# Polysketch attention and feed-forward on one core: GpSimd issues V and all input-projection weights back to back, then the gated query load, in a rebuilt order of work

## The chip, the core and the metric

The kernel runs on one core of a Trainium2 chip. The metric is the device time of one execution in microseconds (us). The kernel before takes 107.55 us, the median of its plain (unprofiled) runs, which all lay between 107.49 and 107.63.

TensorE's clock is granted by a throttle, at full or at half speed. Each run lists its mean granted clock. Three states will turn up:

- *full clock*: full speed begins within the first 7 us and stays until the tail;
- *drop*: it begins early, falls back to half speed for a while before 30 us, and returns;
- *late rise*: full speed begins only at some 20 us.

## The reference, cut to what matters

```python
def phi(x):                                   # q, k, v: 4 batches, 4 heads, 1088 tokens, 32 wide
    a = np.einsum('rd,bhsd->bhsr', S1, x)     # r = 8
    b = np.einsum('rd,bhsd->bhsr', S2, x)
    return np.einsum('bhsi,bhsj->bhsij', a, b).reshape(*x.shape[:-1], r * r)
q_p, k_p = (phi(q), phi(k))
kv = np.einsum('bhsf,bhsd->bhfd', k_p, v)
z = np.sum(k_p, axis=2)
num = np.einsum('bhsf,bhfd->bhsd', q_p, kv)
den = np.einsum('bhsf,bhf->bhs', q_p, z)[..., None] + 1e-06
x = (num / den)                               # heads put side by side: 4352 tokens, 128 wide
h = x @ w_in                                  # to 2048
out = (h * (1.0 / (1.0 + np.exp(-h)))) @ w_out
```

Nothing of the feed-forward can start for a batch until its whole kv and z are there, so the start of the kernel (the *head*) is latency: loads, keys and values of batch 0, then its queries. The rest is a long run of feed-forward matmuls (the *dense part*).

## The kernel before

Every step of the program is an operation with a name. One string, ORDER, sets the order in which they are put out. Each operation goes to a fixed engine (a suffix such as `@DVE` names another one), so ORDER fixes the order within each engine and each queue. `~4:7` means four *fillers*: small matmuls on constant data that keep TensorE busy.

```python
ORDER = """
K0h0 S1 ident tbl0 kvm S2 K0h1 zero mask32 K0h2 tbl Vr0 QA0 E4 Kr0 ~20:7 k0t:0 gateV Kr1 sel@ACT V0
identb@ACT ~1:7 swmm:1 k0e ~1:7 k1t:2 wf:3 k1e@DVE k2t:4 w64 k3t:2 gateQ k2e@DVE k0p:1 k3e wi0 Q0h2
# ... wi1 Q0h0 ... Q0h3 ... wi2 ... Q0h1 ... wi3 ... Q0p ... wo0 ... wo1 ...
Zc0 qAqt:3 KV0r qAm:4 qAqe bz1 KVm0 l2mm:0 wo1 qAaw ntA:3 qArd l2c qArc wo2 xsA QTr00 ~11:7 xtA:3
M0:0 wo3 xA WQm0 ~4:7 L1_A_0:1 QTr01 MQ0 QP0:1,2 qpt:0 QA00 QA01 ~2:4 QM0:1 qpe L1_A_1:0 gate1 Qm0
# ... the rest
"""
```

The names that the argument needs: `wi0` to `wi3` load w_in and `wo0` to `wo3` load w_out, all from GpSimd. `Q0p` loads the queries of four groups of 128 tokens (256 KB), `Q0h0` to `Q0h3` those of three more groups in another layout (48 KB each), all from SyncE. `xA` copies the first activations (tile xT), and `L1_A_0` is the first feed-forward block. `qpt` transposes Q0p; `QTr00` and `QTr01` are VectorE's transposes of Q. `q1`, `q3`, `q5` are the feed-forward chunks of batch 0, made from these queries.

```python
    wl = V0[0]
    for x in WORDER:                          # i0 i1 i2 i3 o0 o1 o2 o3
        ...
        o = dma("POOL", f"w{x}", *d, 256, -9 + 0.1 * len(wi + wo), (), 390.0)
        o.after = [wl]                        # only order within GpSimd's queue
        wl = o
        (wi if x[0] == "i" else wo).append(o)

    def f_gq(s):                              # the gate: QA must have landed
        G_.tensor_copy(out=Q0[:, 0, 0, 0:1], in_=QA[:, 0, 0, 0:1])
        if NPE:
            G_.tensor_copy(out=Q0p[:, 0, 0, 0:1], in_=QA[:, 0, 0, 0:1])
    gq = op("gateQ", "POOL", 0.2 + 0.1 * (NPE > 0), f_gq, QAl, -8.1)
    ...
    def filler(i, n=128):
        mm(bank(i)[:, 0:n], warm, warm)
```

Of the kernel before, what the change touches and what calls it, by code (L numbers as in the profile page):

```python
# [1081 lines left out]
```

## Time and profile before

| | kernel before |
|---|---|
| median of the plain runs | 107.55 us |
| its profiled execution | 110.12 us, span 108.0, mean clock 0.928 (the slow state) |
| w_in issued / landed | 5.20 to 7.3 / 11.30 to 13.88 |
| Q0p issued / landed | 7.05 / 16.80 |
| w_out issued / landed | 9.21 to 11.6 / 14.87 to 17.32 |
| first feed-forward block | 13.88 |
| chunk q1 starts (dense part) | 29.57 |
| dense part, until TensorE's last matmul | 29.57 to 103.11: 73.5 us |

In the lines of the profile, two numbers lead: start and length in us. Then come the engine, the line of the program, the operation, out<-in and the count. A bracket says how long the engine stood idle just before and what ended that. The prediction below quotes the lines for this kernel.

One reading should be kept in mind: the profiled execution was 2.6 us slower than the plain runs and had TensorE at half clock from 13.94 to 27.60.

### The profile page before, as it was taken

The numbers are of one execution on the slowest core, as the hardware profiler recorded it, in microseconds if no ns is written. First come the engines' busy times: TensorE is split into PE (matmuls) and PEld (weight loads), VectorE is DVE, ScalarE is ACT, GpSimd is POOL, SyncE is SP. The second block draws the span as 40 slices with busy tenths as digits, with TensorE's granted clock in tenths as the row PEclk, the third lists the DMA queues.
The fourth block names the chain that finished last, engine by engine and source line by source line (L and its number), as shares of the span: only waits on it lengthen the run. The fifth ranks groups of instructions, "written<-read, shape, count | busy, mean of one in ns | idle before, by whom it ended". The sixth has DMA issues, their size and how long they took to land.

```text
span 108.0 us, 3053 instructions
## 1 busy us (share of the span) xinstructions
PE 98.4 (91%) x1261; PEld 77.1 (71%) x1261; DVE 57.4 (53%) x152; ACT 78.1 (72%) x111; POOL 13.8 (13%) x38
## 2 busy tenths in 40 slices
PE   6999457999999999999999999999999999999910
PEld 6798335998997898664775674877677877779810
DVE  4377240735339789889996697984272040400210
ACT  3474003343599769969999999999898999799800
POOL 7677302000710000050000000000000000000000
PEclk9999955555899999999999999999999999999996
DMA  2999987900299931569935006009720020020211
GB/s 71 182 149 129 233 141 162 242 0 9 54 124 238 202 75 27 128 128 167 245 104 97 6 6 164 0 16 201 178 80 24 0 97 0 6 97 0 97 30 27
DMA packets 20334, 10.62 MB, mean 98 GB/s; under 512 B 11617, under 2 KB 19553, under 8 KB 20321
## 3 DMA queue, kind: packets, MB, share of 16 engines
q1 hardware_dynamic: 15728, 8.20, 31.0%
q0 software_dynamic: 4352, 2.16, 16.9%
q8 instruction: 10, 0.16, 0.7%
q10 hardware_dynamic: 240, 0.07, 0.3%
q14 instruction: 4, 0.02, 0.1%
HBM read 8.79 MB, written 2.23 MB: 102 GB/s over the span
## 4 chain that ended last, share of the span: by engine, by line
PE 77%; DMA 12%; SPq 3%; ACT 3%; issue 1%; POOL 0%; DVE 0%; ACTq 0%
PE ps L709 28%; PE ps L267 18%; PE psAw L267 15%; PE psBw L267 13%; DMA Q0p<-in_q_dram 9%; SPq L272 3%; DMA QA<-in_q_dram 3%; ACT gt L701 2%; PE ps L497 2%; PE ps L782 1%; PE ps L1033 0%; DVE ott L730 0%; ACT ott L732 0%; POOL Q L334 0%; POOL Q0p L336 0%
## 5 line engine op out<-in xcount | busy, mean ns | idle before, releaser
L709 PEld LDWEIGHTS <-gt 128*128 128x128 bf16 x544 | 35.0, 100 | 8.0 <-ACT gt L701 0.4
L709 PE MATMUL ps<-w_out,gt 128*128 128x128 bf16 x544 | 39.3, 222 | 0.2 <-ACT gt L701 0.2
L701 ACT ACTIVATE gt<-psAw 128x1024 bf16<-128x1024 f32 x32 | 32.9, 1029 | 3.0 <-PE psAw L267 2.8
L701 ACT ACTIVATE gt<-psBw 128x1024 bf16<-128x1024 f32 x30 | 30.9, 1029 | 2.1 <-PE psBw L267 1.9
L267 PE MATMUL psBw<-xT,w_in 128*128 128x512 bf16 (+3 forms) x84 | 20.2, 341 | 1.8 <-DVE xT L821 1.8
L267 PEld LDWEIGHTS <-w_in 128*128 128x128 bf16 x176 | 16.9, 117 | 6.6 <-issue 4.4
L267 PE MATMUL psAw<-xT,w_in 128*128 128x512 bf16 (+3 forms) x92 | 21.6, 337 | 0.1
L372 DVE COPY ott<-ps 128x512 f32<-128x512 f32 (+1 forms) x5 | 3.2, 631 | 12.4 <-PE ps L709 7.8
L974 DVE TENSOR_TENSOR qpb<-aqs,AQ 128x512 bf16<-128x512 f32 x12 | 7.8, 682 | 0.1
L427 DVE TENSOR_TENSOR kp<-AB 128x512 bf16<-128x512 f32 x12 | 7.8, 675 | 0.0
L267 PE MATMUL ps<-warm 128*128 128x128 bf16 x56 | 6.6, 279 | 1.0 <-DVE scr L363 1.0
L267 PEld LDWEIGHTS <-warm 128*128 128x128 bf16 x59 | 5.6, 131 | 1.2 <-DVE scr L363 1.0
L372 DVE CAST xT<-ps 128x512 bf16<-128x512 f32 x4 | 2.8, 692 | 6.0 <-PE ps L267 5.8
L370 ACT COPY Q0pT<-ps 128x512 f32<-128x512 f32 x1 | 0.6, 586 | 7.1 <-PE ps L497 7.1
L370 ACT CAST xT<-ps 128x256 bf16<-128x256 f32 (+2 forms) x5 | 2.4, 488 | 2.3 <-PE ps L267 2.3
L941 DVE STREAM_TRANSPOSE QTt<-QL 128x512 f32<-128x512 f32 x6 | 4.0, 692 | 0.0
L699 ACT ACTIVATE gt<-psAw 128x768 bf16<-128x768 f32 x4 | 3.3, 816 | 1.0 <-PE psAw L267 1.0
L267 PE MATMUL ps<-QPTb,KVb 128*128 128x512 bf16 x12 | 3.6, 379 | 0.0
L699 ACT ACTIVATE gt<-psBw 128x768 bf16<-128x768 f32 x4 | 3.3, 814 | 0.0
L272 POOL DMA_DIRECT2D V<-in_v_dram x4 | 3.0, 759 | 0.3 <-POOL V L319 0.3
L948 DVE STREAM_TRANSPOSE AQ<-ps 128x256 f32<-128x256 f32 x6 | 2.4, 426 | 0.8 <-PE ps L267 0.8
L906 DVE STREAM_TRANSPOSE KTt<-KL 128x512 f32<-128x512 f32 x4 | 2.7, 692 | 0.0
(187 smaller groups left out, 116.7 us busy)
## 6 DMA issues: line engine op xcount, KB each, us to landing
QL<-in_q_dram SPq DMA_DIRECT2D x12, 128.0 KB, 4.1
out_dram<-ott SPq DMA_DIRECT2D x6, 256.0 KB, 2.3
V<-in_v_dram POOLq DMA_DIRECT2D x4, 256.0 KB, 5.5
...
```

What stands on the lines that cost most here:

```text
L267: P_.matmul(out_, lhsT, rhs, start=start, stop=stop, **kw)
L272: return op(name, eng, 0.6 if eng == "POOL" else 0.5, lambda s: e.dma_start(dst, src), deps, due, xfer=kb * 1.024 / rate)
L370: A_.copy(out=dst(), in_=src())
L372: V_.tensor_copy(out=dst(), in_=src())
L427: V_.tensor_tensor(out=dst, in0=bcast(a, 2, R), in1=bcast(b_, 1, R), op=ALU.mult)
L699: A_.activation(out=g_[:, 0:2 * n].rearrange("p (a n) -> p a n", a=2), in_=hh[:, :, 0:n], func=ACTF.Silu)
L701: A_.activation(out=g_, in_=hh.rearrange("p a n -> p (a n)"), func=ACTF.Silu)
L709: P_.matmul(ps1[0][:, 128 * u:128 * u + 128], g_[:, n * t + 128 * u:n * t + 128 * u + 128], w_out[:, f, :], start=(f == 0 and u == 0), sto ...
L906: tr.append(op(f"KTr{b}{hf}", "DVE", c_tr(512), lambda s, hf=hf, i=i, b=b: V_.transpose(out=KT[i][:, 2 * hf:2 * hf + 2].rearrange("p j c t ...
L941: tr.append(op(f"QTr{b}{hf}", "DVE", c_tr(512), lambda s, hf=hf, i=i, b=b: V_.transpose(out=QT[i][:, 2 * hf:2 * hf + 2].rearrange("p j c t ...
L948: aqd.append(op(f"QA{b}{P}", "DVE", c_tr(256), lambda s, P=P, b=b, pj=pj: V_.transpose(out=AQ[b][:, :, :, 2 * P:2 * P + 2].rearrange("p x ...
L974: V_.tensor_tensor(out=qp[i][:, hf, g].rearrange("p c h (i j) -> p (c h) i j", j=R), in0=bcast(aqs[i][:, c0:c1, :, 4 * g:4 * g + 4].rearra ...
```

## The change

The intent is to have weights on their way earlier and Q0p in front of the other query loads, with the order of all work rebuilt around that. The computation is the same. The diff, cut to its core:

```diff
 ORDER = """
-K0h0 S1 ident tbl0 kvm S2 K0h1 zero mask32 K0h2 tbl Vr0 QA0 E4 Kr0 ~20:7 k0t:0 gateV Kr1 sel@ACT V0
-identb@ACT ~1:7 swmm:1 k0e ~1:7 k1t:2 wf:3 k1e@DVE k2t:4 w64 k3t:2 gateQ k2e@DVE k0p:1 k3e wi0 Q0h2
+K0h0 S2 ident mask32 S1 K0h1 zero tbl0 K0h2 kvm tbl Vr0 QA0 Kr0 ~20:7 k0t:0 gateV Kr1 V0 ~1:7 swmm:1
+k0e wi0 ~1:7 k1t:2 w64 wf:0 wi1 k1e k2t:3 wi2 k3t:0 k2e@DVE k0p:2 k3e wi3 identb k1p:1 E4 k0c0 sel
+wb4 kqt:0 k0oo gateQ k0c1 k1c0 k2p:3 kqe Q0p k3p:4 k1oo k2c0 Q0h3 kqp:0 k2oo k3c0 k3c1 Q0h2 qb4:2
 ... (every later line changes too)
+wo0 qAqt:2 KV0r qAaw l2mm:1 qAqe wo1 KVm0 qArd l2c ~3:7 ntA:2 qArc wo2 xsA ~9:7 xtA:2 wo3 xA ~8:7
+L1_A_0:1 M0:1 ~1:7 qpt:0 MQ0 L1_A_1:0 qpe S_A_1:0 ~6:7 qpp:0 gate1 Vr1 KL1h2 qpm:2 KL1h0 V1 qpc
+S_A_0:1 QTr00 QL1h0 QTr01 qpaw QL1h2 WQm0 qprd ~9:5 QP0:0,2 QL1h1 L2_A_0:0 qprc QA01 q1as QL1h3 QA00
 ...
-        o = dma("POOL", f"w{x}", *d, 256, -9 + 0.1 * len(wi + wo), (), 390.0)
+        o = dma("POOL", f"w{x}", *d, 256, -9 + 0.1 * len(wi + wo), (), 335.0)
 ...
     gq = op("gateQ", "POOL", 0.2 + 0.1 * (NPE > 0), f_gq, QAl, -8.1)
+    gq.after = [plan.by_name["w" + WORDER[3]]]
```

The number 335 instead of 390 is an estimate for the search that made the order; it has no effect on the chip.

More of the change, by code (lines that the diff above doesn't have):

```diff
@@ L22 @@
 ORDER = """
-K0h0 S1 ident tbl0 kvm S2 K0h1 zero mask32 K0h2 tbl Vr0 QA0 E4 Kr0 ~20:7 k0t:0 gateV Kr1 sel@ACT V0
-identb@ACT ~1:7 swmm:1 k0e ~1:7 k1t:2 wf:3 k1e@DVE k2t:4 w64 k3t:2 gateQ k2e@DVE k0p:1 k3e wi0 Q0h2
-k1p:3 k0c0 wb4 wi1 kqt:2 k0oo Q0h0 k1c1 k3p:4 k1c0 k0c1 Q0h3 kqe wi2 k1oo k2p:0 k3c0 Q0h1 kqp:2 wi3
-k3oo k2c0 k2c1 Q0p qb4:3 qac KV00:1 k2oo k3c1 bz0 qAo0@POOL m8mm:5 krc Z0:4 kr0o mask8 qb4c wo0 KV01
-Zc0 qAqt:3 KV0r qAm:4 qAqe bz1 KVm0 l2mm:0 wo1 qAaw ntA:3 qArd l2c qArc wo2 xsA QTr00 ~11:7 xtA:3
@@ L28 @@
-M0:0 wo3 xA WQm0 ~4:7 L1_A_0:1 QTr01 MQ0 QP0:1,2 qpt:0 QA00 QA01 ~2:4 QM0:1 qpe L1_A_1:0 gate1 Qm0
-S_A_0:0 Vr1 q0aw KL1h2 qpp:1 q0rd KL1h0 q0rc q5as qpm:0 QL1h1 qpc q5qp S_A_1:1 QL1h2 L2_A_0:0 qpaw
-QL1h3 q5qt:2 qprd QL1h0 L2_A_1 qprc q5qe q1as q3as q1qp OT_A ~10:6 q5n:2 q3qp q1qt:0 q5x q1qe@DVE
-~6:6 q3qt:1 gate2 ~1:7 q1n:0 Vr2 q3qe@DVE KL2h2 kk0t:2 q1x Kr3 V1 kk1t:1 kk0e QL2h2 q3n:0 V2
-L1_q1_0:0 kk1e O_A L1_q1_1:1 S_q1_0:1 Kr2 kk0p:1 QL2h0 S_q1_1:0 L1_q1_2:0 KL2h1 kk0c@DVE kk1p:2 Qr2
-QTr10 q3x S_q1_2:2 Qr3 QTr11 L1_q1_3:1 QL2h1 L2_q1_0:0 kk1c@DVE S_q1_3:3 KL2h0 L1_q3_0:0 ko12 KL2h3
@@ L34 @@
-Z1:2 S_q3_0:1 ko11 QP1:0,1 Qr1 Qr0 ko10 L1_q3_1:1 QL2h3 L1_q3_2:0 Zc1 S_q3_1:4 QA11 M1:2 QA10 L2_q1_1
-WQm1 ko13 L2_q1_2 S_q3_2:5 L2_q1_3 QM1:2 OT_q1@DVE KV1:0 Qm1 L1_q3_3:0 Qaw1 L1_q5_0:1 Qrd1 S_q3_3:3
-kr1t:2 L2_q3_0:0 Qrc1 L2_q3_1 Qas1 S_q5_0:2 L2_q3_2 qo101 L1_q5_1:0 kr1e qo100 L2_q3_3 S_q5_1:5
-L1_q5_2:1 KTr20 QD10 qrt:2 OT_q3 kr1p:1 S_q5_2:3 L1_q5_3:0 O_q1 KVt1 kr1c@DVE L2_q5_0:0 KTr21 L2_q5_1
-S_q5_3:4 qo110 L1_q5_4:1 KP2:1,0 S_q5_4:5 L1_q5_5:0 KA21 L2_q5_2 qre@DVE S_q5_5:2 L1_q5_6:1 KVm1
@@ L39 @@
-L2_q5_3 qo111 S_q5_6:3 L2_q5_4 q10n:2 KA20 bz2 QD11 L1_q5_7:0 q10x@DVE L2_q5_5 S_q5_7:5 L2_q5_6 QTr21
-gate3 L1_10_0:1 KL3h1 L1_10_1:0 QTr20 S_10_0:3 KL3h3 Z2:2 QP2:0,1 QL3h2 Zc2 ko23 S_10_1:2 QL3h3 M2:2
-L1_10_2:1 QA20 KL3h0 ko20 L2_q5_7 S_10_2:4 KL3h2 L1_10_3:0 WQm2 bz3 ko22 Vr3 QL3h1 QM2:2 OT_q5 O_q3
-V3 ko21 L1_10_4:1 S_10_3:5 QL3h0 L2_10_0:0 Qm2 L2_10_1 QA21 S_10_4:1 L1_10_5:0 Qaw2 L2_10_2 Qrd2
-S_10_5:2 L1_10_6:1 Qrc2 q11n:0 Qas2 S_10_6:4 L2_10_3 q11x@DVE L1_10_7:0 qo200 L2_10_4 S_10_7:5
@@ L44 @@
-L1_11_0:1 qo201 L2_10_5 S_11_0:1 KTr30 QD20 L1_11_1:0 L2_10_6 KTr31 S_11_1:2 L1_11_2:1 kr1o KP3:0,1
-S_11_2:4 L1_11_3:0 KA30 L2_10_7 KA31 S_11_3:3 L1_11_4:1 KV2:0 S_11_4:5 Z3:1 KVt2 L1_11_5:0 Zc3 KVm2
-qrp:1 QTr30 S_11_5:0 L1_11_6:1 OT_10@DVE M3:0 q20n:2 S_11_6:6 qo211 L2_11_0:0 L1_11_7:0 WQm3 q20x
-qo210 L2_11_1 S_11_7:1 ko32 L1_20_0:1 QD21 L2_11_2 QTr31 O_q5 S_20_0:2 L1_20_1:0 ko33 L2_11_3
-S_20_1:4 ko30 L1_20_2:1 QP3:2,0 qrc S_20_2:3 QM3:1 QA31 QA30 L1_20_3:0 ko31 L1_20_4:1 S_20_3:7 Qm3
-L2_11_4 L2_11_5 Qaw3 S_20_4:5 L1_20_5:0 Qrd3 L2_11_6 Qrc3 S_20_5:0 L2_11_7 Qas3 L1_20_6:1 qo301 OT_11
@@ L50 @@
-q21n:1 qo300 S_20_6:1 L1_20_7:0 qo310 L2_20_0:0 QD30 qrm:0 q21x O_10 L2_20_1 S_20_7:2 O_11 qraw
-L1_21_0:1 qo311 L2_20_2 S_21_0:4 qrrd QD31 L1_21_1:0 qrrc L2_20_3 S_21_1:3 L1_21_2:1 L2_20_4 S_21_2:7
-L1_21_3:0 KV3:0 S_21_3:5 L2_20_5 KVt3 KVm3 L1_21_4:1 L1_21_5:0 S_21_4:0 L2_20_6 L2_20_7 S_21_5:1
-L1_21_6:1 OT_20@DVE q30n:0 S_21_6:2 L1_21_7:0 O_20 q30x@DVE L2_21_0:0 S_21_7:6 qras L2_21_1 qro
-L1_30_0:1 L2_21_2 S_30_0:3 L1_30_1:0 L2_21_3 S_30_1:7 L2_21_4 L1_30_2:1 L1_30_3:0 S_30_2:0 L2_21_5
-L2_21_6 S_30_3:1 L1_30_4:1 qrtt:0 S_30_4:2 L2_21_7 L1_30_5:0 OT_21 q31n:1 L1_30_6:1 S_30_5:6 O_21
@@ L56 @@
-q31x@DVE L2_30_0:0 qree L2_30_1 S_30_6:5 L1_30_7:0 L2_30_2 S_30_7:7 L1_31_0:1 L2_30_3 S_31_0:0
-L1_31_1:0 L2_30_4 S_31_1:1 L1_31_2:1 L2_30_5 S_31_2:2 L2_30_6 L2_30_7 L1_31_3:0 OT_30@DVE L1_31_4:1
-S_31_3:7 qrn:0 O_30 L2_31_0:0 qrx S_31_4:5 L1_31_5:0 L2_31_1 S_31_5:0 L2_31_2 L1_31_6:1 L2_31_3
-S_31_6:2 L1_31_7:0 L2_31_4 S_31_7:7 L1_r_0:1 L2_31_5 S_r_0:5 L1_r_1:0 L2_31_6 S_r_1:0 L2_31_7
-L1_r_2:1 OT_31@DVE L1_r_3:0 S_r_2:7 L2_r_0:0 O_31 L2_r_1 S_r_3:2 L2_r_2 L2_r_3 OT_r0 OT_r1 O_r3 O_r0
-O_r1 O_r2
+K0h0 S2 ident mask32 S1 K0h1 zero tbl0 K0h2 kvm tbl Vr0 QA0 Kr0 ~20:7 k0t:0 gateV Kr1 V0 ~1:7 swmm:1
@@ new lines @@
+k0e wi0 ~1:7 k1t:2 w64 wf:0 wi1 k1e k2t:3 wi2 k3t:0 k2e@DVE k0p:2 k3e wi3 identb k1p:1 E4 k0c0 sel
+wb4 kqt:0 k0oo gateQ k0c1 k1c0 k2p:3 kqe Q0p k3p:4 k1oo k2c0 Q0h3 kqp:0 k2oo k3c0 k3c1 Q0h2 qb4:2
+k1c1 k2c1 krc m8mm:1 k3oo bz0 Q0h1 qac bz1 Z0:3 mask8 qAo0@POOL qb4c KV00:5 Q0h0 Zc0 KV01 kr0o qAm:3
+wo0 qAqt:2 KV0r qAaw l2mm:1 qAqe wo1 KVm0 qArd l2c ~3:7 ntA:2 qArc wo2 xsA ~9:7 xtA:2 wo3 xA ~8:7
+L1_A_0:1 M0:1 ~1:7 qpt:0 MQ0 L1_A_1:0 qpe S_A_1:0 ~6:7 qpp:0 gate1 Vr1 KL1h2 qpm:2 KL1h0 V1 qpc
+S_A_0:1 QTr00 QL1h0 QTr01 qpaw QL1h2 WQm0 qprd ~9:5 QP0:0,2 QL1h1 L2_A_0:0 qprc QA01 q1as QL1h3 QA00
@@ new lines @@
+QM0:1 q1qp q3as q1qt:0 q3qp L2_A_1 q1qe Qm0 ~2:7 q3qt:2 OT_A q0aw q1n:0 q0rd ~3:6 kk0t:1 q1x q0rc
+q3qe q5as L1_q1_0:1 q5qp kk0e kk1t:0 L1_q1_1:0 kk1e@DVE q3n:2 S_q1_1:0 q5qt:1 q3x@DVE kk0p:0 q5qe@DVE
+S_q1_0:1 q5n:1 kk1p:2 QTr10 q5x QTr11 gate2 L1_q1_2:1 V2 KL2h1 kk0c@DVE L1_q1_3:0 S_q1_2:2 kk1c@DVE
+KL2h0 QP1:0,1 ko13 KL2h3 Z1:2 S_q1_3:3 Kr3 ko11 L1_q3_0:1 Kr2 L2_q1_0:0 Zc1 S_q3_0:4 ko12 M1:2 Qr0
+L2_q1_1 ko10 KL2h2 L1_q3_1:0 O_A QA11 L2_q1_2 S_q3_1:0 WQm1 QA10 QL2h3 L1_q3_2:1 QL2h0 QM1:2 S_q3_2:2
@@ new lines @@
+KV1:0 Qm1 L2_q1_3 Qaw1 L1_q3_3:1 Qrd1 OT_q1 L1_q5_0:0 Qrc1 O_q1 S_q3_3:3 L2_q3_0:0 Qas1 QL2h1 L2_q3_1
+qo101 S_q5_0:4 QL2h2 L2_q3_2 qo100 L1_q5_1:1 kr1t:2 L2_q3_3 S_q5_1:2 kr1e@DVE QD10 KVt1 L1_q5_2:0
+OT_q3@DVE kr1p:0 Qr2 S_q5_2:3 L1_q5_3:1 KTr21 L2_q5_0:0 KTr20 L2_q5_1 S_q5_3:0 L1_q5_4:0 qo111
+KP2:2,1 S_q5_4:2 KVm1 L2_q5_2 KA20 L1_q5_5:1 KA21 L1_q5_6:0 S_q5_5:3 qo110 L2_q5_3 q10n:1 S_q5_6:0
+QD11 L1_q5_7:1 q10x@DVE L2_q5_4 S_q5_7:4 L2_q5_5 QTr20 gate3 L1_10_0:0 kr1c KL3h3 L1_10_1:1 QTr21 bz2
@@ new lines @@
+S_10_0:3 QL3h2 Z2:0 ko20 QP2:1,2 KL3h0 S_10_1:2 Zc2 KL3h1 kr1o L1_10_2:0 QA20 M2:0 KL3h2 S_10_2:1
+L2_q5_6 QA21 QL3h0 L1_10_3:1 WQm2 ko21 L2_q5_7 Qr3 S_10_3:0 L1_10_4:0 ko23 Qr1 QM2:0 ko22 QL3h1
+S_10_4:4 q11n:1 QL3h3 bz3 Vr3 L1_10_5:1 O_q3 OT_q5 q11x@DVE L1_10_6:0 Vr2 S_10_5:5 Qm2 L2_10_0:0 V3
+Qaw2 L2_10_1 S_10_6:3 Qrd2 L1_10_7:1 L2_10_2 Qrc2 S_10_7:2 L1_11_0:0 Qas2 L2_10_3 S_11_0:1 KTr31
+L2_10_4 L1_11_1:1 KTr30 L2_10_5 S_11_1:4 qo200 L1_11_2:0 L2_10_6 qo201 S_11_2:5 L2_10_7 qo211 QD20
+L1_11_3:1 OT_10 qo210 KP3:0,1 S_11_3:2 QTr30 L1_11_4:0 QD21 L2_11_0:0 O_10 KA31 L1_11_5:1 KA30 O_q5
@@ new lines @@
+QTr31 Z3:0 S_11_5:1 KV2:1 Zc3 QP3:0,2 KVt2 S_11_4:3 KVm2 L1_11_6:1 ko33 q20n:1 S_11_6:0 QA31
+L1_11_7:0 q20x@DVE L2_11_1 S_11_7:6 QA30 L2_11_2 ko30 L1_20_0:1 L2_11_3 ko32 S_20_0:5 L1_20_1:0 M3:0
+qrt:2 S_20_1:2 WQm3 L1_20_2:1 ko31 q21n:1 S_20_2:4 L1_20_3:0 q21x@DVE L2_11_4 S_20_3:7 L2_11_5
+L1_20_4:1 qre L2_11_6 S_20_4:1 L1_20_5:0 L2_11_7 S_20_5:0 QM3:2 OT_11@DVE KV3:1 Qm3 L1_20_6:0 Qaw3
+L1_20_7:1 Qrd3 S_20_6:6 L2_20_0:0 Qrc3 L2_20_1 Qas3 S_20_7:5 L1_21_0:0 qo300 L2_20_2 S_21_0:2 qo301
+L2_20_3 L1_21_1:1 QD30 L2_20_4 S_21_1:7 L1_21_2:0 L2_20_5 S_21_2:1 L1_21_3:1 qrp:2 S_21_3:0 L1_21_4:0
@@ new lines @@
+qrc@DVE KVt3 L2_20_6 qo310 S_21_4:4 L2_20_7 KVm3 qrm:1 OT_20@DVE L1_21_5:1 qraw L1_21_6:0 S_21_5:5
+q30n:2 L2_21_0:0 q30x@DVE S_21_6:6 L1_21_7:1 qo311 L2_21_1 S_21_7:2 L1_30_0:0 qrrd QD31 qrrc L2_21_2
+qras O_11 S_30_0:7 L2_21_3 O_20 L1_30_1:1 L2_21_4 S_30_1:0 L1_30_2:0 L2_21_5 S_30_2:4 L2_21_6 L2_21_7
+L1_30_3:0 OT_21@DVE q31n:2 S_30_3:2 qro L1_30_4:1 O_21 L2_30_0:0 S_30_4:6 L1_30_5:0 q31x@DVE L2_30_1
+S_30_5:7 L1_30_6:1 qrtt:1 L2_30_2 S_30_6:0 qree L1_30_7:0 L2_30_3 S_30_7:4 L1_31_0:1 L2_30_4 S_31_0:2
@@ L62 @@
+L1_31_1:0 L2_30_5 S_31_1:6 L1_31_2:1 L2_30_6 S_31_2:7 L2_30_7 L1_31_3:0 OT_30@DVE qrn:1 S_31_3:4
+L1_31_4:1 qrx L2_31_0:0 S_31_4:0 L1_31_5:0 L2_31_1 S_31_5:2 L2_31_2 L1_31_6:1 L2_31_3 S_31_6:7
+L1_31_7:0 L2_31_4 S_31_7:4 L1_r_0:1 L2_31_5 S_r_0:0 L1_r_1:0 L2_31_6 S_r_1:2 L2_31_7 L1_r_2:1
+OT_31@DVE L1_r_3:0 S_r_2:4 L2_r_0:0 O_31 L2_r_1 O_30 S_r_3:7 L2_r_2 L2_r_3 OT_r1 OT_r0 O_r3 O_r2 O_r1
+O_r0
 """
```

## The prediction

> **What bounds the kernel now.** I read the page first (span, slices), then the chain of waits for the first 34 us, then the timeline of that stretch, then busy time by stage. The page's slices (2.7 us each) come first:
>
> ```profile
> PE   6999457999999999999999999999999999999910
> ...
> PEclk9999955555899999999999999999999999999996
> DMA  2999987900299931569935006009720020020211
> ```
>
> Two kernels stand in this one. From the eleventh slice on (about 30 us) TensorE is busy nine tenths or more at full clock until the tail. Before it, slices 5 and 6 show TensorE at 4 and 5 tenths, then seven tenths and more at a clock of 0.5. The DMA engines are full in slices 2 to 9. So the steady part can only become shorter through less TensorE work, and the head through an earlier start. The chain that ended last, for the head:
>
> ```profile
> 7.05 9.75 DMA Q0p<-in_q_dram
> 16.80 0.14 issue
> 16.93 1.08 PE ps L497 x4
> 18.02 0.69 PE ps L267 x10
> 18.71 0.97 PE psAw L267 x8
> 19.68 3.36 PE ps L267 x16
> ...
> 29.57 0.44 PE psAw L267 x4
> ```
>
> One load, Q0p (queries of four token groups, 256 KB), is issued at 7.05 and lands at 16.80. Everything after hangs on it: its transposes, the first feed-forward block put between (18.71), its sketch and denominator products (19.68 to 23.04), and at 29.57 the first two-group feed-forward chunk, q1, with which the dense part begins. The timeline says why the load is late and what else stands still:
>
> ```profile
> 5.18 1.77 SPq L272 DMA_DIRECT2D Q<-in_q_dram  x4
> 5.20 2.14 POOL L272 DMA_DIRECT2D w_in<-in_moe_w_in_dram  x4
> ...
> 7.05 0.39 SPq L272 DMA_DIRECT2D Q0p<-in_q_dram  x1
> ...
> 13.34 0.38 DVE L864 STREAM_TRANSPOSE Q0T<-Q 128x192 f32<-128x192 f32 x1 [2.00 <-DMA Q<-in_q_dram]
> 13.64 0.19 DVE L821 COPY xT<-psB 128x128 bf16<-128x128 bf16 x1
> ...
> 13.88 0.98 PE L267 MATMUL psBw<-xT,w_in 128*128 128x128 bf16 x8 [1.83 <-DVE xT L821]
> ```
>
> SyncE puts four smaller query loads (Q, 48 KB each) ahead of Q0p in its queue. GpSimd issues the four input-projection pieces only at 5.20, after a gate that waited for QA; it had finished issuing V at 4.26. VectorE stands 2.00 us in a transpose that waits for Q, and behind it waits the copy that makes the first activations (xT). TensorE idles 1.83 us for that copy. The busy time by stage shows the price in clock:
>
> ```profile
> 10.00:14.00 4.00, 2.17 (x26) 1.77 (x27) 1.73 (x9) 0.58 (x2) 1.61 (x4) 0.99 1.19 216
> 14.00:17.00 3.00, 1.43 (x25) 0.91 (x24) 0.83 (x4) 0.00 (x0) 0.83 (x2) 0.50 0.62 102
> ...
> 24.00:27.60 3.60, 3.60 (x33) 3.26 (x31) 1.67 (x6) 1.53 (x3) 0.00 (x0) 0.50 0.02 7
> ...
> 36.00:44.00 8.00, 8.00 (x148) 6.57 (x146) 6.68 (x16) 6.30 (x10) 0.20 (x1) 1.00 0.55 102
> ```
>
> The columns are stretch, length, then busy us of TensorE, its weight load, VectorE, ScalarE and GpSimd, then clock, DMA share and GB/s. TensorE is busy 2.17 of 4.00 us before 14 and 1.43 of 3.00 after it, and its clock is half from 14.0 to 27.6. From 36 on it is the bound (8.00 of 8.00; VectorE 6.68, ScalarE 6.30).
>
> **What the Trainium skill says.** "DMA: Bandwidth & Descriptors", section "Issuing engines are not separate DMA queues", says that loads from SyncE and GpSimd share the same 16 engines and interleave. Its section "Queues, rings and completion order" says that within a queue descriptors are taken in ring order, and that an engine alternates between queues. The trace agrees: the last Q load (issued 6.52, up to 6.7 us to landing) comes in at 13.2, Q0p 3.6 us later, though it was issued just 0.5 us after it. So place in SyncE's queue decides which query load is early, not the issue time alone. "TensorE: Matmul & The Clock Gate", section "What's actually happening", says that TensorE's clock is halved when it was not busy enough in a window of 3413 ns. The trace agrees: clock 0.50 follows on the thin stretch, and the 13.6 us of it are four such windows. How busy a window must be, neither tells me.
>
> **The change, part by part.** No arithmetic is removed. The order of instructions on each engine, which I compared for both kernels, shows four things.
>
> *One: GpSimd.* After V come the four w_in issues directly, then the two gate copies. w_in starts at 4.26 and not 5.20, 0.94 us earlier. The gate is done at 4.26 + 2.14 + about 0.35 = 6.75, so Q0p is issued at about 6.8, 0.25 us earlier. The pieces took 6.1 to 7.1 us to land (11.3 to 13.9); I take 0.9 us off: 10.4 to 13.0.
>
> *Two: SyncE.* Q0p is now first, the four Q loads follow it. Q's first share landed no sooner than 11.4 and the last at 13.2, 6.2 to 8.0 us after the first Q issue at 5.18. A Q0p in that place, beside the same weights, should land about 7 us after its issue: 13.9, by 2.9 us earlier. The price: Q gets Q0p's old place and lands at about 16.3.
>
> *Three: VectorE.* The transposes of Q now stand behind xT, so the first activations are ready when their transpose is (11.63 in the trace, plus 0.19 and some delay: 11.9, not 13.83). The first feed-forward block starts near 12.0 instead of 13.88; w_in's first two pieces (11.3) allow it. The Q transposes are ahead of Q0p's denominator instead, which ties this chain to Q's landing: 16.3 + 0.75 for the two transposes = 17.1.
>
> *Four: TensorE.* 63 warm-up fillers instead of 56, eight of them between the last head transpose and the first block, so the stretch before 14 is denser. Chunk q1 goes ahead of q5, which was first before.
>
> The chain from Q0p, at full clock (and at half clock in brackets). Landing 13.9 plus 0.14 issue. Four transposes: 1.08 us at half clock, 0.55 by half of that: 14.6 (15.1). Copy by ScalarE 0.59: 15.2 (15.7). Sketch product: 1.91 at half clock; the same eight passes for batch 1 took 1.00 at 30.28, at full clock: 16.2 (17.6). Denominator product 1.86 at half clock: 17.1 (19.5); the tie with Q's transposes is at 17.1 too. VectorE's denominator, scaling and outer product for q1 took 23.15 to 25.03, plus three small operations now between, 0.17 + 2 x 0.23: 2.5 us: 19.6 (22.0). Transposes, copy, numerator and copy for q1: about 0.3 + 0.6 + 0.3 + 0.4 = 1.6 (1.9): 21.2 (23.9). Then chunk q1 starts, against 29.4 in the profile of before.
>
> That is 8.2 (5.5) us earlier. Not all is gain: q5's transposes and numerator, q3's numerator and half of batch 1's key transposes, which stood ahead of q1, now stand behind it: about 0.36 + 0.32 + 0.2 + 0.5 = 1.4 us of TensorE at full clock. Left are 6.8 (4.1) us, since the dense part behind is TensorE-bound and its loads (V1 is now issued at the first gate) and VectorE's batch-1 work move forward with it. One more deduction: the profiled run took 110.12 us and the plain runs 107.55. The dense matmuls run at full clock in the profile, so I think those 2.6 us sit in the head, as half-clock windows that plain runs have fewer of. Taking 0 to 2.6 off gives gains from 1.5 to 6.8, with the middle near 4.1; I take off another half a microsecond for new gaps in a rebuilt order, which gives 3.6 and so 103.9 us.
>
> **The rivals.** *Q takes Q0p's place as the bound.* For it: the DMA engines are full until 16.2 and the same bytes have to move; Q's transposes are ahead of Q0p's denominator on VectorE. Against: its chain at 16.3 ties with the other and is not behind. If Q lands at 17.5 and not 16.3, 1.2 us of gain are lost: about 105. *The load is hidden anyway.* If Q0p still lands near 16, because weights and queries share the engines, only the first block ahead of it (0.97 us) and q1's place ahead of q5 are won, 1 to 2 us: about 106, within 2%. *The clock.* If TensorE still drops to half at 14, bracketed numbers hold: 104.5 to 106. If the denser stretch keeps it full and plain runs of before had most of the half-clock time too, the time could be 101.5. *The dense part refuses the gain:* batch 1's keys, V1 and queries all load at the first gate now and could come late for TensorE, giving 105 to 106. Against it: the DMA engines have room there (share 0.34 from 20 to 24 us, 0.02 from 24.0 to 27.6).
>
> **Range and chances.** Predicted 103.9 us; 8 times in 10 between 101.8 and 106.2. Two per cent faster is 105.4. Every part of the head points forward, and only a late Q0p or a crowd of two rivals together keeps it above 105.4: faster 0.77, same 0.20. Slower by 2% would need the rebuilt order to open gaps in the dense part: 0.03.
>
> **What would show it.** Right: w_in issues from 4.3; Q0p issued before Q and landing by about 14; xT and the first block at 12; q1's first block 5 us or more earlier; the dense part as long as before plus about 1.4 us. Wrong: Q0p landing after 15.5; VectorE waiting in Q's transposes past 17.5; clock 0.5 from 14 to 27 again; a DMA wait on TensorE after 20 us; or an end that moves much less than q1's start.

## The result, and the profile after

| | before | after |
|---|---|---|
| plain and profiled runs (us) | 107.63, 107.55, 107.49, 107.54 | 103.28, 104.41, 103.84, 104.59 |
| median | 107.55 | 104.12 |
| ratio of fast runs | | 0.967, 95% interval 0.961 to 0.974 |
| profiled execution | 110.12, clock 0.928 | 103.28, clock 1.0 |

A ratio here is roughly the mean time of one kernel's fast runs over that of the other kernel's fast runs in the same rounds, so it is not quite the ratio of the medians. The clocks of before's four plain runs were not recorded.

So the change won 3.3%, close to the forecast. The slices of the changed kernel's page (2.5 us each) look as the prediction hoped, with no half clock shown. (The clock row counts from the first clock record, here at 6.29 us; before it, the transposes of K took some 420 ns each, against 272 in a_again at full clock. More on that at a_q0p_last.)

```profile
PE   6999999899999997999999999999999999999920
...
PEclk9999999999999999999999999999999999999999
DMA  3999993980496464699339100005009300000331
```

The timeline of the head shows the parts of the change at work:

```profile
4.27 2.16 POOL L272 DMA_DIRECT2D w_in<-in_moe_w_in_dram  x4
...
6.87 0.38 SPq L272 DMA_DIRECT2D Q0p<-in_q_dram  x1
...
7.29 2.05 SPq L272 DMA_DIRECT2D Q<-in_q_dram  x4
...
12.71 0.23 DVE L822 COPY xT<-psB 128x128 bf16<-128x128 bf16 x1 [0.32 <-PE psB L820]
...
12.99 0.61 PE L267 MATMUL psBw<-xT,w_in 128*128 128x128 bf16 x8
...
13.69 0.60 PE L498 MATMUL ps<-ident,Q0p 128*128 128x128 f32 x4
```

w_in is issued at 4.27, and its four pieces took 4.3 to 5.4 us to land (6.1 to 7.1 before). Q0p is issued before Q, and its transposes start at 13.69 without waiting for anything. xT comes at 12.71, no longer behind Q. The chain of waits runs almost wholly through TensorE:

```profile
14.74 2.21 PE ps L267 x22
17.00 0.04 issue
17.05 0.29 DVE aw L750
...
18.46 0.58 DVE qp L428
19.04 0.05 issue
19.09 0.40 PE ps L783 x4
...
21.18 0.45 PE psBw L267 x4
```

The last of these lines is chunk q1, at 21.18 instead of 29.57. (The chain counts a matmul only from the end of the one before it, so its starts lie up to 0.2 us behind those of a timeline.) But the busy time by stage, with the columns that the prediction explains, shows that the dense part has become worse:

```profile
36.00:44.00 8.00, 7.19 (x104) 4.55 (x105) 6.64 (x17) 6.38 (x10) 2.53 (x6) 1.00 0.62 128
```

Before, TensorE was busy 8.00 of these 8.00 us. TensorE's timeline names the wait:

```profile
39.03 0.38 PE L267 MATMUL ps<-QPTb,KVb 128*128 128x512 bf16 x1 [0.70 <-DMA QPTb<-qpb]
```

This is the numerator of batch 1. It waits 0.70 us for a transposing DMA.

The account between the two recorded executions: the head is 29.57 - 21.18 = 8.4 us shorter. The dense part runs from 21.18 to 97.12, which is 75.9 us, 2.4 longer. The tail behind TensorE's last matmul is 0.6 us shorter (101.4 - 97.12 = 4.3 against 108.0 - 103.11 = 4.9). 8.4 - 2.4 + 0.6 = 6.6 us, the difference of the spans. This account compares an execution at full clock with one that had 13.6 us at half clock. The experiments had to separate the two.

### The profile page after: what moved, and what is told of

Its sections match the earlier page's. It is cut to its first block, busy times and chain, and to the rows that moved or that the text cites. A ratio compares the mean times of both kernels' runs of the same rounds, so it can differ in the third digit from the quotient of the medians.

```text
span 101.4 us, 3049 instructions
## 1 busy us (share of the span) xinstructions
PE 93.7 (92%) x1256; PEld 74.3 (73%) x1268; DVE 59.5 (59%) x157; ACT 76.0 (75%) x106; POOL 14.0 (14%) x38
## 3 DMA queue, kind: packets, MB, share of 16 engines
q0 software_dynamic: 4352, 2.16, 17.1%
## 4 chain that ended last, share of the span: by engine, by line
PE 75%; DVE 7%; DMA 4%; SPq 4%; ACT 4%; issue 2%; POOL 0%; ACTq 0%; DVEq 0%
PE ps L710 25%; PE ps L267 18%; PE psAw L267 11%; PE psBw L267 11%; DMA QL<-in_q_dram 4%; SPq L272 4%; ACT gt L702 3%; DVE qpb L975 2%; PE psA L267 2%; PE ps L498 2%; PE psB L267 1%; DVE KTt L907 1%; PE ps L783 1%; PE psB L535 1%; PE psA L535 1%
## 5 line engine op out<-in xcount | busy, mean ns | idle before, releaser
L710 PEld LDWEIGHTS <-gt 128*128 128x128 bf16 x544 | 34.2, 98 | 8.6 <-ACT gt L702 0.4
L702 ACT ACTIVATE gt<-psBw 128x1024 bf16<-128x1024 f32 x31 | 31.8, 1026 | 3.9 <-PE psBw L267 3.7
L702 ACT ACTIVATE gt<-psAw 128x1024 bf16<-128x1024 f32 x31 | 31.8, 1026 | 3.4 <-PE psAw L267 1.7
L267 PE MATMUL psAw<-xT,w_in 128*128 128x512 bf16 (+3 forms) x81 | 19.4, 332 | 0.1
L267 PE MATMUL psBw<-xT,w_in 128*128 128x512 bf16 (+3 forms) x84 | 19.2, 323 | 0.1
L373 DVE COPY ott<-ps 128x512 f32<-128x512 f32 (+1 forms) x6 | 3.9, 647 | 15.8 <-PE ps L710 15.7
L373 DVE CAST xT<-ps 128x512 bf16<-128x512 f32 (+1 forms) x7 | 4.6, 653 | 3.1 <-PE ps L267 1.7
L267 PEld LDWEIGHTS <-KVb 128*128 128x128 bf16 x18 | 1.3, 97 | 2.1 <-DVE qpb L975 0.8
L371 ACT COPY QPT<-ps 128x512 bf16<-128x512 bf16 x2 | 1.2, 589 | 2.1 <-PE ps L783 2.1
L272 POOL DMA_DIRECT2D Vr<-in_v_dram x4 | 2.6, 660 | 0.0
```

Of the source, the lines that this page charges most:

```text
L267: P_.matmul(out_, lhsT, rhs, start=start, stop=stop, **kw)
L272: return op(name, eng, 0.6 if eng == "POOL" else 0.5, lambda s: e.dma_start(dst, src), deps, due, xfer=kb * 1.024 / rate)
L371: A_.copy(out=dst(), in_=src())
L373: V_.tensor_copy(out=dst(), in_=src())
L702: A_.activation(out=g_, in_=hh.rearrange("p a n -> p (a n)"), func=ACTF.Silu)
L710: P_.matmul(ps1[0][:, 128 * u:128 * u + 128], g_[:, n * t + 128 * u:n * t + 128 * u + 128], w_out[:, f, :], start=(f == 0 and u == 0), sto ...
```

## The experiments

Twelve kernels ran. The theory at the start was the prediction's own: Q0p's earlier landing is the gain. The rival: the gain is only a matter of clock states.

### Controls: both kernels again, unaltered

**a_again** is the changed kernel without an edit, **b_again** the kernel before without an edit.

> The changed kernel once more, unaltered, as the measure for the three runs beside it. Median near 104.1 us, spread about 1.3 us as in its first four runs; clock 0.99 or more. If the time of single runs depends on when the clock first rises (6.3 us in the first profile of it, 3.7 us in the profile of before), a profile with an early rise has all its head work about 0.7 us sooner.

> The kernel before, unaltered, for the states of its runs and a profile of another state than the first (110.12 us, clock 0.5 from 14 to 27.6). Theory Clock (all that the change gains is TensorE's clock in the head): runs with a recorded clock of 0.99 or more and an early first rise take 103.0 to 103.6 us, as the changed kernel does; every 0.01 of clock less costs about 1 us. In a profile of such a run chunk q1 starts near 23 us and the dense part is about 2.5 us shorter than in the changed kernel. Rival Load (the earlier Q0p gains by itself): runs of full clock still take 105 or more.

a_again ran 103.28, 103.15 and 102.80, and twice slow (107.61, 109.17), where a spread of 1.3 us was expected. Against the kernel before in the same rounds the ratio of fast runs is 0.998, interval 0.990 to 1.006: no gain. b_again ran 102.86, 102.95, 102.24, 102.48, 103.46, and once slow (109.13, clock 0.942). The kernel "of 107.55 us" thus runs in 102 to 103.5 us whenever its clock holds. Its profiled execution of 102.86 us was such a one. The clock row of the page, then its chain of waits:

```profile
PEclk9999999999999999999999999999999999999995
```

```profile
13.47 0.61 PE psBw L267 x8
14.08 0.33 PE ps L267 x16
14.41 0.58 PE ps L497 x4
...
15.97 1.87 PE ps L267 x16
...
22.33 0.44 PE psAw L267 x4
```

At full clock the kernel *before* starts the first block at 13.47 and Q0p's transposes at 14.41 (Q0p landed at 14.19, not 16.80). Sketch and denominator products take 1.87 us, not 3.36. Chunk q1 starts at 22.33, not 29.57. The change has only 22.33 - 21.18 = 1.15 us left to win in the head, less than the 1.4 us of work that it moves from ahead of q1 to behind it. And the dense part of before, busy by stage:

```profile
36.00:44.00 8.00, 7.89 (x113) 4.78 (x115) 7.14 (x16) 6.80 (x10) 1.76 (x4) 1.00 0.77 142
```

It runs from 22.33 to 95.87: again 73.5 us, as in the half-clocked execution. So at equal clock the account reads 1.15 us won in the head, 2.4 lost in the dense part, 0.4 won in the tail (4.3 against 4.7): 0.8 us longer, which is what the spans of these two executions say (101.4 against 100.6).

The profile of a_again shows why a shorter head is worth so little. It is the same kernel, but its clock rose earlier (4.57 us and not 6.29), and its q1 started at 20.32 where the first profile's timeline has 21.02:

```profile
20.32 0.60 PE L267 MATMUL psBw<-xT,w_in 128*128 128x256 bf16 x4
...
24.23 1.30 DVE L942 STREAM_TRANSPOSE QTt<-QL 128x512 f32<-128x512 f32 x2 [1.23 <-DMA QL<-in_q_dram]
...
25.90 0.67 PE L267 MATMUL ps<-QTt,Wp 64*32 64x256 f32 x16 [0.56 <-DVE AB L373]
```

QL holds the queries of batch 1. In both executions VectorE waits for that load, to 24.23 here and 24.33 there, and TensorE's products of it start at 25.90 and 26.00. The load in turn is issued behind a copy on GpSimd that waits for w_out to land (15.26 here, 15.47 there). So a head that is 0.70 us shorter brought nothing: both executions took 103.28 us.

The kernel before ran 37 times. Sorted by time and clock:

| state | runs | times (us) | mean clock |
|---|---|---|---|
| full clock | 18 | 101.99 to 103.59, mean 102.91 | 0.984 to 1.0 |
| drop | 14 | 104.38 to 110.91 | 0.925 to 0.974 |
| late rise | 5 | 107.52 to 107.76 | 0.985 to 0.986 |

The mean of all is 105.39 us. The changed kernel, unaltered, has nine runs in all: no drop, two late rises, mean 104.68.

The states other than those of profiled executions are inferred from time and clock, and no profile of the kernel before fell on a late rise. The inference for the late rise rests on the next experiment.

### a_q0p_last: Q0p behind the other query loads

```diff
-... kqe Q0p k3p:4 k1oo k2c0 Q0h3 ... Q0h2 ... Q0h1 ... Q0h0 Zc0 ...
+... kqe k3p:4 k1oo k2c0 Q0h3 ... Q0h2 ... Q0h1 ... Q0h0 Q0p Zc0 ...
```

> The changed kernel with Q0p put behind the four Q loads in SyncE's queue, nothing else. My prediction's theory (Q0p's place in SyncE's queue decides): Q0p lands about 2 us later than it does, its transposes start at 15.5 or later instead of 13.7, the time is 1.5 to 2.5 us longer, near 106. Rival (the weights queued ahead of all query loads drain the DMA engines early, so that all five query loads are in by 13.5 whatever their order): Q0p lands at about 13.4, its transposes start within 0.3 us of 13.7, the time is that of the control within 0.5 us.

Measured: 102.94, 103.26, 103.02, 103.00, and one slow run of 109.04, the profiled one. Ratio to before 0.999 (0.995 to 1.003), like a_again's. The place of Q0p in SyncE's queue is worth nothing. The view of this tile says why:

```profile
L498 PE MATMUL ps<-ident,Q0p x4: 421/421/421, 18.4 to 19.1; 128*128 128x128 f32 x4
...
L272 SPq DMA_DIRECT2D Q0p<-in_q_dram x1: 385/385/385, 8.6 to 8.6; - x1
...
DMA to landing us min/median/max: 4.2/4.2/4.2
```

Issued last, at 8.59, Q0p landed 4.2 us later, at 12.80. Q had landed by 12.17. All five query loads come in close together: the order of the queue holds, but being last costs 0.6 us and not the 3.6 that the prediction read from the trace of before. (This is the slow execution; no fast one of this variant was profiled.)

The same lines show the late rise. The transposes last 421 ns each. In the changed kernel's fast execution they last 272:

```profile
L498 PE MATMUL ps<-ident,Q0p x4: 272/272/278, 13.7 to 14.0; 128*128 128x128 f32 x4
```

In this slow execution the trace's first clock record is at 20.28, and TensorE ran at half clock until then. Yet its stage table says:

```profile
17.00:20.00 3.00, 3.00 (x25) 2.94 (x24) 0.85 (x3) 0.48 (x1) 1.54 (x3) 1.00 0.62 144
```

The clock column reads 1.00 (third from the right), because it counts only from the first record. So a run of 107 us and more with a mean clock near 1 is not at full clock from the start. Durations of one matmul form tell.

### a_gate_first: the gate ahead of w_in again

```diff
-k0e wi0 ~1:7 k1t:2 ... k0oo gateQ k0c1 ...
+k0e gateQ wi0 ~1:7 k1t:2 ... k0oo k0c1 ...
-    gq.after = [plan.by_name["w" + WORDER[3]]]
```

> The changed kernel with the gate copies put back ahead of the four w_in issues on GpSimd, nothing else. Theory that the back-to-back issue matters by itself: w_in is issued from 5.2, shares the engines with Q0p and Q, the last piece lands at 13.9 instead of 11.3, the second feed-forward block and all behind it wait 0.5 to 1 us: about 105. Rival (only the order built around it matters): Q0p is issued at 5.2 and is in by 11, the last w_in piece by 13.9 is just in time for the block at 14.1, and the time is that of the control within 0.5 us.

Measured: 104.23, 103.94, 105.10, 103.82, and a late rise of 108.98 (profiled, first record at 20.38). Ratio to before 1.011 (1.002 to 1.020). w_in was issued from 5.30 and landed at 10.61 to 13.33. The fast runs average 104.27, those of a_again 103.08: the back-to-back issue may be worth about 1 us within the changed order. That is not shown clear of noise: the two intervals overlap, and the changed kernel itself had runs of 104.4 and 104.6.

### a_no_fill: the changed order without its later fillers

Eight groups of fillers behind the opening are dropped, 41 in all; nothing else is edited.

```diff
-... l2c ~3:7 ntA:2 ... xsA ~9:7 xtA:2 ... xA ~8:7
-L1_A_0:1 M0:1 ~1:7 qpt:0 ... ~6:7 qpp:0 ... ~9:5 QP0:0,2 ... ~2:7 q3qt:2 ... ~3:6 kk0t:1
+... l2c ntA:2 ... xsA xtA:2 ... xA
+L1_A_0:1 M0:1 qpt:0 ... qpp:0 ... QP0:0,2 ... q3qt:2 ... kk0t:1
```

> The changed kernel without its last 41 warm-up fillers (those between 11 and 21 us). Theory that the clock carries much of the gain: a profile shows a granted clock of 0.5 for three or four windows from about 14 us, chunk q1 starts 1.5 to 3 us later, the time is 106 to 107. Rival (the real matmuls suffice, as TensorE no longer waits 1.8 us for xT and 1.6 us for Q0p): clock stays 0.99 or more, the time is that of the control within 0.5 us.

Measured: 103.57, 107.15, 103.30, 103.44, 101.96, with clocks 0.976, 0.929, 0.977, 0.992, 0.997. Three of five runs are below 0.98, and the profiled one shows half clock from 18.16 to 21.57. Drops are back, though milder than expected: the profile has one stretch of 3.41 us at half clock and not three or four, and the ratio is 0.997 (0.984 to 1.011). Within the changed order the fillers bring the steady clock. What they cost is open: the one run at 0.997 took 101.96, 1.1 us less than the mean of a_again's fast runs.

### b_fill: the kernel before with more fillers

```diff
-M0:0 wo3 xA WQm0 ~4:7 L1_A_0:1 QTr01 MQ0 QP0:1,2 qpt:0
+M0:0 wo3 xA WQm0 ~32:7 L1_A_0:1 QTr01 MQ0 QP0:1,2 ~26:4 qpt:0
```

> The kernel before with 28 more warm-up fillers ahead of the first feed-forward block and 26 more ahead of Q0p's transposes, where TensorE stood idle for 1.83 and 1.57 us; no load, order or gate changed. Theory Clock: no run drops to half clock between 14 and 28 us (recorded clock 0.99 or more in all), the typical run takes 103.0 to 103.8, as the changed kernel does; what is left of slow runs are those whose clock first rises only near 20 us (107 to 109). Rival Load: the times stay where those of before are, since Q0p still lands at 16.8.

Measured: 104.70, 104.58, 104.36, 104.66, 104.81, clocks 0.988 to 0.992, and one late rise of 110.74 (profiled, first record at 20.10). Ratio 1.017 (1.011 to 1.024). No drop in six runs: 54 fillers alone, in the old order, seem to hold the clock (at before's rate of drops, 14 in 37, six runs without one have a chance of 6%). There were too many of them, and they cost 1.7% of the full-clock time, more than was expected.

### b_xt_first: only the transpose of Q moved behind xT

```diff
-... xsA QTr00 ~11:7 xtA:3
-M0:0 wo3 xA WQm0 ~4:7 L1_A_0:1 ...
+... xsA ~11:7 xtA:3
+M0:0 wo3 xA QTr00 WQm0 ~4:7 L1_A_0:1 ...
```

> The kernel before with one VectorE instruction moved: the first transpose of Q stands behind the copy that makes xT. The first feed-forward block starts near 12.3 us (then it waits for the second w_in piece) and not at 13.9. My prediction counted this start as part of the gain. Theory Clock: nothing but Q0p's landing (16.8) sets the chain, so runs of full clock take 103.0 to 103.6 as before; fewer runs drop to half clock, as a wait of 1.8 us is gone, but the wait for Q0p grows by 1.6. Rival (the early block is worth something): full-clock runs are 0.5 to 1 us faster than those of before.

Measured: 103.45, 102.71, 103.63 at full clock; 106.64 and 106.97 with clocks of 0.954 and 0.957; 107.53 with 0.986. Ratio 1.004 (0.993 to 1.015). An earlier first block is worth nothing at full clock, since the idle time of TensorE only moves: 0.88 us behind the block, for the transposes of Q, and 0.99 us more, for Q0p, which landed at 15.02. Drops remain.

### a_long_warm: a longer opening burst

```diff
-... Kr0 ~20:7 k0t:0 ...
+... Kr0 ~42:7 k0t:0 ...
```

> The changed kernel with 42 fillers in its opening burst in place of 20. If the slow runs of the changed kernel (107.6 to 109.2 at a recorded clock of 0.99) are those in which the first 20 us ran at half clock because the opening burst filled no activity window, a burst of more than 5 us ends them: all runs within 1.5 us of each other, at 103.1 plus what the burst delays the first transposes, 1.4 to 2.5 us, so 104.5 to 105.6. Rival (something else makes those runs slow, as a late load): slow runs of 109 us and more remain.

Measured: 103.68, 104.08, 104.42, 103.95, 103.42, 102.90, none of them slow. Ratio 1.009 (1.000 to 1.017). The changed kernel and those of its variants that keep both its opening and its fillers had 4 late rises in 19 runs; here there was none in 6. That fits an opening burst that was too short, but six runs cannot prove it. Nor can it be the whole cause: in a_q0p_last TensorE was busy nine tenths and more of every slice from 2.7 us on, long after the burst, and full clock still came only at 20.28. The burst costs about 0.7 us (mean 103.74 against 103.08 for a_again's fast runs), half of what was expected or less, and the mean of *all* runs is lower than that of a_again's five: 103.74 against 105.20.

### c_wo_late and c_wo_xt: why before drops

What brings the kernel before to half clock? Comparing its two profiled executions gave an idea. In the one with the drop the clock had risen at 3.70. Everything was early, including the issue of w_out from GpSimd:

```profile
9.21 0.59 POOL L272 DMA_DIRECT2D w_out<-in_moe_w_out_dram  x1
```

In b_again, where the clock rose at 5.83, it came a microsecond later:

```profile
10.26 0.59 POOL L272 DMA_DIRECT2D w_out<-in_moe_w_out_dram  x1
```

Q0p landed at 16.80 in the first case and at 14.19 in the second, though its issue times (7.05 and 7.43) hardly differ. In b_xt_first, with w_out at 9.21 as well, it landed at 15.02. An early w_out, it seems, gets in front of Q0p's data, though it cannot explain all of the delay, since 15.02 and 16.80 go with the same 9.21. c_wo_late holds w_out back with one small copy on GpSimd; c_wo_xt adds the move of b_xt_first.

```diff
+    op("gateW", "POOL", 0.2, lambda s: G_.tensor_copy(
+        out=w_out[:, 0:1, 0:1].rearrange("p a b -> p (a b)"), in_=w_in[:, 0:1]), [wi[0]], -6)
 ...
-... qb4c wo0 KV01 ...
+... qb4c gateW wo0 KV01 ...
```

> The kernel before, with one small copy added on GpSimd that reads the first landed piece of w_in, ahead of the four issues of w_out. In the profile of before that fell to half clock, w_out was issued at 9.21 and Q0p landed only at 16.80; in the one at full clock w_out was issued at 10.26 and Q0p landed at 14.19. Theory W (w_out overtakes Q0p, TensorE runs dry between the first feed-forward block and Q0p, and that idle time brings the half clock): w_out is issued from about 11, Q0p lands by 14.5 whatever the clock of the first microseconds, and the runs with a drop to half clock (about 10 in 26 of before) become rare: at most one of the six. Rival D (the first gap, 1.8 us in which TensorE waits for xT behind the transposes of Q, brings it on alone): Q0p lands early and 2 or more of the six still show a clock under 0.975. Under both the fast runs stay at 102.2 to 103.5.

> The kernel before with both small edits: w_out held behind the first landed piece of w_in, and the first transpose of Q moved behind xT on VectorE. No filler is added. Both theories of the drop then expect none: each of the two gaps ahead of 17 us shrinks to under 1 us, clocks of 0.98 and more, fast runs of 102.3 to 103.8. If drops remain (2 or more of six under 0.975), they don't hang on these two gaps but on something that neither edit touches, such as the place of the activity windows alone.

c_wo_late: 102.75, 103.31, 102.15, 102.65, 102.91, and one drop (106.66, clock 0.953). c_wo_xt: 102.63, 101.86, 102.61, 102.26, 102.48, and one run of 107.52 with clock 0.986, by its numbers a late rise. Ratios 1.001 (0.995 to 1.007) and 0.997 (0.993 to 1.002). In the same rounds the kernel before had 4 drops, 3 late rises and 4 fast runs. The profiled c_wo_xt had its clock at 4.25, early, and yet:

```profile
10.95 0.59 POOL L272 DMA_DIRECT2D w_out<-in_moe_w_out_dram  x1 [0.30 <-POOL w_out L337]
...
14.13 0.63 PE L498 MATMUL ps<-ident,Q0p 128*128 128x128 f32 x4 [0.20 <-DMA Q0p<-in_q_dram]
```

w_out goes out at 10.95, Q0p lands at 14.00, and TensorE waits 0.20 us for it, where it waited 1.57 before. In the 12 runs of the two kernels there is one drop; at before's rate of 14 in 37 one would expect 4.5. With w_out held back, Q0p comes in early and drops become rarer. How the one leads to the other is not shown. In the profile of before the half clock begins at 13.94, ahead of the wait for Q0p (15.36 to 16.93), so that wait cannot have begun it. Just before it lies the wait for xT, which hangs on the landing of Q, and c_wo_late shortened that one as well, from 1.83 us to 0.77; so its rival D is not excluded. Whether the second edit is needed beside it, one drop in six against none in six does not tell.

### c_b_best: both edits, a longer opening, six more fillers

```diff
 (the edits of c_wo_xt, and)
-... Kr0 ~20:7 k0t:0 ... xA QTr00 WQm0 ~4:7 L1_A_0:1
+... Kr0 ~30:7 k0t:0 ... xA QTr00 WQm0 ~10:7 L1_A_0:1
```

> The kernel before with both small edits, the opening burst of 30 fillers instead of 20, and 10 instead of 4 fillers ahead of the first feed-forward block; nothing else of the change. Expected 102.6 to 103.6 us in every run, clocks from 0.985, neither drops to half clock nor a first rise at 20 us. Then the robustness that the change buys is to be had without rebuilding the order, and the mean of all runs is 2 us and more below that of before. If runs of 107 and more remain, 30 fillers are too few for the opening or the drop has another cause.

Measured: 103.35, 105.16, 103.69, 103.89, 103.43, 104.31, clocks 0.988 to 1.0. There is no run at 107, and no clock that speaks of a drop; the run of 105.16 counts as slow, at a clock of 0.999, and is not explained. But the fast runs are 1.2% slower than before's (ratio 1.012), so the expectation held only in part: four of the six lie above its range. All six runs average 103.97, those of before in these rounds 105.55, so the gain of the mean is 1.6 us, not 2.

### c_best: the changed kernel with three repairs

```diff
-... Kr0 ~20:7 k0t:0 ... xA ~8:7 L1_A_0:1 ... ~6:7 qpp:0 ... ~9:5 QP0:0,2 ... ~2:7 q3qt:2 ... ~3:6 kk0t:1
+... Kr0 ~30:7 k0t:0 ... xA ~5:7 L1_A_0:1 ... ~3:7 qpp:0 ... ~4:5 QP0:0,2 ... q3qt:2 ... kk0t:1
-... L2_q5_3 q10n:1 S_q5_6:0 QD11 L1_q5_7:1 q10x@DVE L2_q5_4 S_q5_7:4 L2_q5_5 QTr20 gate3 ...
+... L2_q5_3 S_q5_6:0 QD11 L1_q5_7:1 L2_q5_4 q10n:1 q10x@DVE S_q5_7:4 L2_q5_5 QTr20 L2_q5_6 gate3 ...
```

Although 16 fillers are gone (the expectation says 20, a miscount), the point of the experiment is the same.

> The changed kernel with three repairs: the opening burst of 30 fillers instead of 20, 20 of the later fillers ahead of q1 taken out, and the numerator of the first half of batch 1 moved behind two more matmul groups, so that its wait for the DMA transpose of QPT (0.70 to 0.84 us) is covered. Expected: that gap falls under 0.2 us and q1 starts about 0.5 us earlier or at the same time (fillers that lay in waits give nothing), so fast runs of 101.8 to 102.7 against 102.8 to 103.3 of the unaltered change, with no run at a late first rise (107 and more). If the fast runs stay at 103 the dense part gives the time back later, as it gave back the earlier start.

A miss. Measured: 103.70, 103.27, 104.88, 104.84, 104.90, 106.76; the ratio, from the first two alone, is 1.008 (1.003 to 1.013). TensorE's timeline of the 103.70 us execution:

```profile
38.97 0.48 PE L267 MATMUL psBw<-xT,w_in 128*128 128x384 bf16 x2 [0.62 <-ACT gt L700]
```

The wait for the transposing DMA is gone, and at the same place TensorE waits 0.62 us for ScalarE's activations instead. The repaired wait had lain on top of another one: in the first profile of the changed kernel the activation of that place ends at 38.90 too (38.09 plus 0.81). The run of 106.76 has a clock of 0.981. The runs of 104.8 to 104.9 have clocks of 0.991 to 0.997 and fit neither a drop nor a rise at 20 us; no profile fell on one, so what they are stays open.

## Why the prediction was right or wrong

The forecast was 103.9 us and the result 104.12, inside the range and in the right class. The number was right, and the reason given for it mostly was not. The fit is luck: a net gain in the head that was not there at equal clock, and a base of 107.55 us that by all signs was not the kernel's full-clock time, made up for each other.

Two readings in the prediction are off. The DMA row that it shows is at 7 to 9 in slices 2 to 8 and at 0 in slice 9, so "full in slices 2 to 9" is one slice too many; and "full until 16.2" does not agree with its own stage table, where the share is 0.62 from 14 to 17.

**Part one, GpSimd: right.** w_in was issued at 4.27 (predicted 4.26) and Q0p at 6.87 (about 6.8). The pieces landed at 8.53 to 11.31, sooner than the 10.4 to 13.0 of the forecast, because each took 4.3 to 5.4 us instead of the 6.1 to 7.1 that were carried over. a_gate_first put about 1 us on it, within noise.

**Part two, "place in SyncE's queue decides which query load is early": wrong.** Q0p was indeed early (transposes from 13.69; 13.9 plus 0.14 was predicted), but Q landed at 12.68 to 13.43 and not at 16.3. Putting Q0p last in the queue (a_q0p_last) did not change the time, and Q0p still landed at 12.80. What went with the late Q0p in the profile of before was w_out from the other queue: c_wo_xt held that back and left SyncE's order alone, and Q0p landed at 14.00. But b_xt_first, with w_out as early as there, had it at 15.02, so part of the delay stays unexplained. The tie of the chain to Q's landing at 17.1 therefore never came about.

**Part three, VectorE: right in order, worth nothing.** xT left its place behind Q's transposes. It came at 12.71, not 11.9, and the first block at 12.99, because that execution's clock rose only at 6.29; a_again had the block at 12.28. b_xt_first shows that the early block alone saves no time.

**Part four, TensorE: the start was hit, the comparison missed.** q1 started at 21.18; predicted 21.2. The moved 1.4 us stands up: the pieces now behind q1 are, in b_again's chain, half of the eight transposes of 0.87 us, and q5's transposes and numerators of about 0.9 us. But the start was compared with the 29.4 us of an execution that had half clock in it. The step that failed is the deduction: "Taking 0 to 2.6 off". The half clock in the head of before was worth 29.57 - 22.33 = 7.2 us (b_again), not at most 2.6. With 7.2 in its place the sum is 8.2 - 7.2 - 1.4 - 0.5, about 1 us *lost*; b_again and the changed kernel differ by 0.8 in span, and a_again's ratio is 0.998.

The half microsecond "for new gaps in a rebuilt order" was about right. The 2.4 us by which the dense part grew are the moved 1.4, the new wait of 0.70, and 0.3 that I have not traced. That the dense part would grow by the moved work was forecast. What the prediction had wrong is "its loads [...] move forward with it": batch 1's queries came no earlier when the head was shorter (a_again), and TensorE waited 0.56 us for their products there.

**Where the 3.3% came from, then.** All four runs of before in the first call took 107.5 us. Not one of its 18 full-clock runs takes more than 103.6, so by that measure those four were slow. (Time was part of the sorting, but the clock agrees: of the 23 later runs with a clock of 0.984 or more, 18 took up to 103.6 and the other five 107.5 to 107.8.) Which state it was stays open, for their clocks were not recorded. Their narrow spread (0.14 us) and their level resemble the five late rises (107.52 to 107.76), but one drop run of 107.75 stands there as well, and the profiled execution was a drop. The changed kernel's four runs happened to have no late rise. Had both been compared over many runs, the difference of the means would have been about 0.7 us (105.39 and 104.68), from few runs of the changed kernel.

**The rivals.** *The clock* was named as a rival, with the right idea that plain runs of before might have most of the half-clock time too. That was the decisive one, and it got too little weight. *The load is hidden anyway* came true in another sense: at full clock Q0p lands at 14.19 in the kernel before. *The dense part refuses the gain* came true: 2.4 us longer, with a DMA wait on TensorE after 20 us, as the prediction's list of signs says. *Q as the bound* did not.

**What the change does buy.** Its fillers leave TensorE nothing to wait for between 1 and 17 us (busy 15.83 of these 16.00). With them there was no drop in 19 runs (the changed kernel, a_q0p_last, a_gate_first); without them (a_no_fill) three of five runs had a lowered clock. The same is, it seems, to be had without the rebuilt order. c_wo_xt, two small edits to the kernel before, had no drop in six runs, a median of 102.54 us and the lowest mean of all the kernels tried (103.23, its slow run included). It did not run in the same rounds as the changed kernel, and against before's fast runs its ratio of 0.997 is no gain either: it, too, only makes the good state more frequent, as far as six runs can tell.

## What to carry to other kernels

Before crediting a change with a shorter chain, compare two executions in the same clock state; run the old kernel often enough to know its states, and check a suspicious clock share against the duration of one fixed matmul form. A kernel with a thin head can win more from holding its clock than from an earlier load, and a load from another queue that goes out too early may be part of what takes the clock away. When one wait is covered and the time does not move, look for the wait that lay beneath it.

## What the Trainium skill lacked or had wrong

- "TensorE: Matmul & The Clock Gate", section "What's actually happening", puts the warm-up at about 3.4 us of busy time, with a varying phase, and calls its cost small. Here the first rise came at 3.70 to 6.53 us in some profiled executions and at 20.10 to 20.38 in three others, though in one of these, a_q0p_last, TensorE was busy nine tenths and more in every slice from 2.7 to 24 us. The late rise costs 4.5 to 6 us of 103.
- The same page's section "HAM oscillation — how this bites in real kernels" gives as its abstract rule that idle gaps must stay under about 3.4 us. In the kernel before two gaps of 1.83 and 1.57 us (the first ends at 13.88, the second lies within the half clock) came with half clock from 13.94 to 27.60, and in a_no_fill gaps of at most 0.52 us came with half clock from 18.16 to 21.57. So half clock came with much shorter idle stretches than one window; that they caused it is not shown. The page's next section, "A second HAM failure mode: psum-queue depth-cycling", does say that frequent micro-idles make the clock swing, but gives no size.
- Beyond a warning on the same page ("Seeing it yourself") that the clock's trace events can be unreliable, no page that I read says that a mean granted clock may leave out the time before the first record. In a_q0p_last it reads 0.994 while the matmuls of 17 to 20 us ran at half speed (421 ns instead of 272).
- "DMA: Bandwidth & Descriptors", section "Queues, rings and completion order", gives the round of an engine through its queues, but not what a queue's late load then costs. Here one load of 256 KB (Q0p) took 9.7 and 8.0 us where another queue's w_out (four pieces, 128 KB each where they land) began to be issued 2.2 us after it, 6.7 to 7.5 us where that began 2.8 us or more after it, and 4.2 us where the input weights had been queued well ahead of it.
